# A linear-attention normaliser moved from TensorE products to VectorE block transposes

## The chip, the cores and the metric

The kernel runs on one core of one Trainium2 chip. The metric is the device time of the slowest core, here the only one, in microseconds (us). PE is TensorE, PEld its weight loads, DVE VectorE, ACT ScalarE, POOL GpSimd, SP SyncE.

## The reference, cut to what matters

```python
qkv = (x @ wqkv) ...                     # 32 heads of 16, S = 2048, D = 512
pq, pk = phi(q), phi(k)                  # phi(t) = where(t > 0, t + 1, exp(t)) + 1e-6
kv = einsum("bhsd,bhse->bhde", pk, v)
z = einsum("bhsd->bhd", pk)
num = einsum("bhqd,bhde->bhqe", pq, kv)
den = einsum("bhqd,bhd->bhq", pq, z)[..., None] + 1e-6
a = (num / den) ... @ wo
b = ...                                  # token-mixing MLP: layernorm, w1, gelu, w2
return g * a + (1 - g) * b               # g = sigmoid((x * gate_w).sum(-1))
```

The change touches `den`: one number per head and query. It is the sum of 16 products, the 16 features of that head times the head's column of sums `z`.

## The kernel before

All large products go through PE. Their names in the profile are `kacc` and `qacc` (k and q), `gacc` (phi(k)^T x), `uacc` (the first MLP product, 14 f-tiles of 16 matmuls), `aps` (attention output, 4 matmuls a tile of 128 queries) and `yps` (second MLP product, 14 a tile). Between two uacc f-tiles three short groups run: `kvps` (kv), `denps` (the normaliser) and `w2ps` (kv times Wo).

`pqT` holds phi(q) with features on the partitions, in four feature blocks j and four chunks c of 512 queries. The normaliser is a product with a masked column of sums, `Z32`. Its reciprocal then has to be spread from one row per head to 16 rows, and that was done by a round trip through DRAM:

```python
    def den_matmuls():
        denps = bank("denps")
        for j in range(ND):
            for c in range(NSC):
                mm(denps[32 * c : 32 * c + 32, :], Z32[:, 32 * j : 32 * j + 32],
                   pqT[:, j, c * SC : (c + 1) * SC],
                   j == 0, j == ND - 1, tile_position=(0, 32 * c))
        with nc.allow_low_precision(reason="the normalizer is used in bf16"):
            nc.vector.reciprocal(out=rden[:], in_=denps[:])
    ...
    def rden_chunk(c):
        if c == 0:
            nc.gpsimd.dma_start(out=rd_dram[:], in_=rden[:])
        for j in range(ND):
            rex = work.tile([P, SC], BF16, name="rex", tag="rex", bufs=4)
            src = rd_dram[32 * c + 8 * j : 32 * c + 8 * j + 8, :]
            nc.gpsimd.dma_start(out=rex[:], in_=src.unsqueeze(1).to_broadcast([8, HEAD, SC]))
            seg = pqT[:, j, c * SC : (c + 1) * SC]
            nc.vector.tensor_tensor(out=seg, in0=seg, in1=rex[:], op=ALU.mult)
    ...
    for j in range(NB0, NF):            # f-tiles 3 to 13
        ...                             # 16 uacc matmuls, then gelu on ACT
        if j == NB0 + 3:
            kv_matmuls(); den_matmuls(); w2_matmuls()
            gate_sums(); rden_chunk(0); rden_chunk(1)
        if NB0 + 3 <= j < NB0 + 3 + ND:
            w2_copies(j - NB0 - 3)
    ...
    for t in range(NT):                 # 16 tiles of 128 queries
        ...                             # aps, a_sc (ACT), yps, ot (DVE)
        (nc.scalar if t < 2 else nc.sync).dma_start(out=o_view[:, t, cs], in_=ot[:, :W])
        if 0 < t < NSC - 1:
            rden_chunk(t + 1)
```

`w2_matmuls` needs `kvT`, which DVE makes from `kvps` (a masked copy). PSUM has eight banks in this kernel's pool, two per tile in the last stage.

## Time and profile before

| | before |
|---|---|
| time, median of 3 runs | 164.11 us (164.09 to 164.12) |
| span of the profiled run | 162.3 us |
| PE / DVE / ACT busy | 97% / 55% / 39% |

The page of the kernel before: the line of busy times (engine, us, share of the span, instructions) and the shares by engine of the chain that ended last.

```profile
PE 157.7 (97%) x819; PEld 72.2 (45%) x833; DVE 90.0 (55%) x211; ACT 62.8 (39%) x96; POOL 17.5 (11%) x34
...
PE 94%; DMA 3%; issue 1%; ACTq 1%; DVE 0%
```

PE is busy nearly all the time (97%), and nearly the whole chain is PE (94%). A change elsewhere can be expected to gain nothing by itself.

The chain of waits of the kernel before, where the short groups run (start us, us, what):

```profile
66.26 4.91 PE uacc L113 x22
71.17 0.59 PE kvps L113 x64
71.76 0.88 PE denps L113 x16
72.65 0.36 PE w2ps L113 x16
73.01 0.32 PE uacc L113
```

PE leaves uacc at 71.17 and is back at 73.01. The 16 denps matmuls take 0.88 us of that. `kvT` is made meanwhile, so w2ps need not wait for it.

The groups of instructions of the kernel before on DVE that serve to cost the change (line, engine, operation, tile, shapes, count, busy us, mean ns, idle time before it):

```profile
L446 DVE TENSOR_TENSOR pqT<-pqT,rex 128x512 bf16<-128x512 bf16 x16 | 6.2, 421 | 3.9 <-DMA rex<-rd_dram 3.7
...
L404 DVE RECIPROCAL rden<-denps 128x512 bf16<-128x512 f32 x1 | 3.4, 3358 | 0.5 <-PE denps L113 0.5
...
L355 DVE STREAM_TRANSPOSE zT<-zacc 128x512 f32<-128x512 f32 x1 | 0.7, 711 | 0.0
L356 DVE TENSOR_REDUCE zpart<-zT 128x16 f32<-128x512 f32 x1 | 0.7, 686 | 0.0
```

A 128x512 fp32 block transpose and a sum over short runs are already in the kernel, once each. They give 711 and 686 ns for the new code, which does each 16 times. The reciprocal over 512 columns takes 3358 ns.

### The profile page before, as it was taken

How to read it: one execution, taken by the hardware profiler on the slowest of the kernel's cores; microseconds unless marked ns; L12 is line 12 of the kernel's file. 1: busy time of each engine (PE TensorE's matmuls, PEld its weight loads, DVE VectorE, ACT ScalarE, POOL GpSimd, SP SyncE). 2: the span in 40 equal slices, each digit the busy share in tenths (PEclk: the TensorE clock that was granted, in tenths of full speed). 3: DMA queues.
4: the chain of work that ended last, by engine and by line, in shares of the span. 5: the costliest groups of instructions: out<-in, count | busy, mean ns of one | idle time of the engine just before them, and what ended most of it. 6: DMA issues, size and time to landing. Idle time of an engine off the chain costs nothing.

```text
span 162.3 us, 2175 instructions
## 1 busy us (share of the span) xinstructions
PE 157.7 (97%) x819; PEld 72.2 (45%) x833; DVE 90.0 (55%) x211; ACT 62.8 (39%) x96; POOL 17.5 (11%) x34
## 2 busy tenths in 40 slices
PE   7999999999999999999999999999999999999993
PEld 3344444444444444444444444444444444444452
DVE  1799999957999999519995301256211111111112
ACT  3362486648676483112865113111222222111110
POOL 3000710200100000001505500050000000000000
DMA  5999999999900007500892599832000001110001
GB/s 149 203 249 259 288 295 352 377 387 387 345 18 0 0 0 247 205 4 0 290 316 86 203 299 324 298 129 72 32 32 32 32 32 43 48 42 33 32 32 32
DMA packets 30569, 25.18 MB, mean 155 GB/s; under 512 B 8480, under 2 KB 29984, under 8 KB 30560
## 3 DMA queue, kind: packets, MB, share of 16 engines
q1 hardware_dynamic: 28256, 21.89, 43.3%
q0 software_dynamic: 1440, 2.38, 5.5%
q10 hardware_dynamic: 864, 0.79, 1.5%
q8 instruction: 6, 0.10, 0.2%
q14 instruction: 3, 0.02, 0.0%
HBM read 21.11 MB, written 2.23 MB: 144 GB/s over the span
## 4 chain that ended last, share of the span: by engine, by line
PE 94%; DMA 3%; issue 1%; ACTq 1%; DVE 0%
PE uacc L113 30%; PE yps L113 30%; PE aps L113 8%; PE qacc L113 8%; PE gacc L113 8%; PE kacc L113 8%; DMA wk_sb<-in_A_wqkv_dram 3%; PE denps L113 1%; ACTq L129 1%; PE kvps L113 0%; PE w2ps L113 0%; DVE ot L505 0%; PE pt L335 0%
## 5 line engine op out<-in xcount | busy, mean ns | idle before, releaser
L113 PE MATMUL uacc<-hs,w1c 128*128 128x512 bf16 x220 | 51.1, 379 | 0.2
L113 PE MATMUL yps<-uT,w2c 128*128 128x512 bf16 (+2 forms) x234 | 50.6, 366 | 0.2
L505 DVE SCALAR_TENSOR_TENSOR ot<-yps,c,a_sc 128x512 bf16<-128x512 f32 (+2 forms) x17 | 12.2, 720 | 45.0 <-PE yps L113 41.8
L113 PEld LDWEIGHTS <-w2c 128*128 128x128 bf16 x238 | 22.8, 98 | 25.9
L113 PEld LDWEIGHTS <-w1c 128*128 128x128 bf16 x224 | 21.8, 98 | 26.3 <-issue 0.2
L492 ACT ACTIVATE a_sc<-aps,c,gg 128x512 f32<-128x512 f32 x16 | 12.4, 778 | 46.7 <-PE aps L113 39.9
L329 ACT ACTIVATE uT<-uacc,bcol 128x512 bf16<-128x512 f32 x14 | 9.3, 688 | 21.7 <-PE uacc L113 21.6
L113 PE MATMUL kacc<-wk_sb,xT 128*128 128x512 bf16 x63 | 16.1, 380 | 0.3
L113 PE MATMUL qacc<-xT,wq_sb 128*128 128x512 bf16 x61 | 16.1, 379 | 0.2
L113 PE MATMUL aps<-W2sb,pqT 128*128 128x512 bf16 x63 | 16.2, 379 | 0.1
L113 PE MATMUL gacc<-pk,xs 128*128 128x512 bf16 x63 | 15.6, 379 | 0.0
L256 ACT ACTIVATE hs<-xs,nmr,rstd 128x512 bf16<-128x512 bf16 x16 | 12.8, 805 | 1.8 <-DVE nmr L250 1.8
L216 ACT ACTIVATE e<-qacc 128x512 bf16<-128x512 f32 x16 | 9.6, 597 | 9.2 <-PE qacc L113 9.2
L216 ACT ACTIVATE e<-kacc 128x512 bf16<-128x512 f32 x16 | 9.3, 594 | 9.2 <-PE kacc L113 9.1
L444 POOL DMA_DIRECT2D rex<-rd_dram x16 | 9.5, 599 | 22.5 <-DVE pqT L446 19.4
L220 DVE SCALAR_TENSOR_TENSOR pk<-kacc,e 128x512 bf16<-128x512 f32 x16 | 11.1, 691 | 0.6
L220 DVE SCALAR_TENSOR_TENSOR pqT<-qacc,e 128x512 bf16<-128x512 f32 x16 | 11.1, 692 | 0.6
L113 PEld LDWEIGHTS <-xs 128*128 128x128 bf16 x76 | 7.2, 102 | 8.5 <-DMA xs<-in_A_x_dram 0.8
L240 DVE BATCH_NORM_STATS2 stats<-xs 128x6 f32<-128x512 bf16 x16 | 10.9, 682 | 0.0
L217 DVE TENSOR_SCALAR e<-e 128x512 bf16<-128x512 bf16 x32 | 9.0, 281 | 3.0 <-ACT e L216 3.0
L431 DVE CUSTOM_DVE_ANT_0 junk<-xs,gw_b 128x512 bf16<-128x512 bf16 x16 | 9.8, 681 | 0.0
L113 PEld LDWEIGHTS <-xT 128*128 128x128 bf16 x64 | 6.1, 97 | 8.2 <-DVE xT L212 0.6
(61 smaller groups left out, 73.0 us busy)
## 6 DMA issues: line engine op xcount, KB each, us to landing
w2c<-in_B_w_dram SPq DMA_DIRECT2D x8, 896.0 KB, 6.7
w1c<-in_B_w_dram SPq DMA_DIRECT2D x2, 2048.0 KB, 14.0
w1c<-in_B_w_dram SPq DMA_DIRECT2D x3, 1024.0 KB, 11.9
rex<-rd_dram POOLq DMA_DIRECT2D x16, 128.0 KB, 3.7
out_dram<-ot SPq DMA_DIRECT2D x13, 128.0 KB, 1.7
xs<-in_A_x_dram SPq DMA_DIRECT2D x3, 512.0 KB, 4.7
wq_sb<-in_A_wqkv_dram SPq DMA_DIRECT2D x1, 512.0 KB, 6.5
wv_sb<-in_A_wqkv_dram SPq DMA_DIRECT2D x1, 512.0 KB, 12.2
```

What stands on the lines that cost most here:

```text
L113: nc.tensor.matmul(o, lhsT=lhsT, rhs=rhs, start=start, stop=stop, **kw)
L129: q.dma_start(out=xs[:, t0 : t0 + n, :], in_=x_view[:, t0 : t0 + n, :])
L216: nc.scalar.activation(out=e[:], in_=acc[:], func=ACT.Exp)
L217: nc.vector.tensor_scalar(out=e[:], in0=e[:], scalar1=1.0, scalar2=PHI_EPS, op0=ALU.min, op1=ALU.add)
L220: nc.vector.scalar_tensor_tensor(out=dst, in0=acc[:], scalar=0.0, in1=e[:], op0=ALU.max, op1=ALU.add)
L240: nc.vector.bn_stats(out=stats[:], in_=xs[:, t, :])
L256: nc.scalar.activation(out=hs[:, t, :], in_=xs[:, t, :], func=ACT.Identity, scale=rstd[:, t : t + 1], bias=nmr[:, t : t + 1],)
L329: nc.scalar.activation(out=uT[:, j, :], in_=acc[:], func=ACT.Gelu_apprx_tanh, bias=bcol[:, j : j + 1])
L431: nc.vector.tensor_tensor_reduce(out=junk[:], in0=xs[:, t, :], in1=gw_b[:], scale=1.0, scalar=0.0, op0=ALU.mult, op1=ALU.add, accum_out=gp ...
L444: nc.gpsimd.dma_start(out=rex[:], in_=src.unsqueeze(1).to_broadcast([8, HEAD, SC]))
L492: nc.scalar.activation(out=a_sc[:], in_=aps[:], func=ACT.Identity, scale=gg[:, t : t + 1], bias=c2[:, t : t + 1],)
L505: nc.vector.scalar_tensor_tensor(out=ot[:, :W], in0=yps[:, :W], scalar=c1[:, t : t + 1], in1=a_sc[:, cs], op0=ALU.mult, op1=ALU.add,)
```

## The change

The intent is to take the normaliser off PE and off the DRAM round trip. ACT multiplies `pqT` by the column of sums, feature by feature. DVE transposes 32x32 blocks, so that the 16 features of a head lie side by side in one row; it sums runs of 16, takes the reciprocal of 32 columns, and transposes a broadcast view back, which spreads each reciprocal over 16 partitions. The work comes in 16 blocks (c, j): six during the uacc f-tiles and ten in the first ten query tiles. `kv_matmuls` moves one f-tile earlier, and `w2_matmuls` stays, now one f-tile behind it. The 16 gate sums on DVE, one block of work before, are spread over eight f-tiles, two in each.

```diff
-    def den_matmuls():
-        ...
+    def den_block(c, j):
+        seg = pqT[:, j, c * SC : (c + 1) * SC]
+        pz = work.tile([P, SC], FP32, name="pz", tag="pz", bufs=2)
+        nc.scalar.activation(out=pz[:], in_=seg, func=ACT.Copy, scale=zcol[:, j : j + 1])
+        nc.vector.transpose(out=zT[:], in_=pz[:])
+        den = work.tile([P, SC // HEAD], FP32, name="den", tag="den", bufs=1)
+        nc.vector.tensor_reduce(
+            out=den[:], in_=zT[:].rearrange("p (a d) -> p a d", d=HEAD), op=ALU.add, axis=AX.X
+        )
+        rd = work.tile([P, SC // HEAD], BF16, name="rd", tag="rd", bufs=1)
         with nc.allow_low_precision(reason="the normalizer is used in bf16"):
+            nc.vector.reciprocal(out=rd[:], in_=den[:])
+        rex = work.tile([P, SC], BF16, name="rex", tag="rex", bufs=1)
+        nc.vector.transpose(
+            out=rex[:].rearrange("p (a d) -> p a d", d=HEAD),
+            in_=rd[:].unsqueeze(2).to_broadcast([P, SC // HEAD, HEAD]),
+        )
+        nc.vector.tensor_tensor(out=seg, in0=seg, in1=rex[:], op=ALU.mult)
 ...
-        if j == NB0 + 3:
+        i = j - NB0
+        if i == 2:
             kv_matmuls()
-            den_matmuls()
+        elif i == 3:
             w2_matmuls()
-            gate_sums()
-            rden_chunk(0)
-            rden_chunk(1)
-        if NB0 + 3 <= j < NB0 + 3 + ND:
-            w2_copies(j - NB0 - 3)
+        if 3 <= i < 3 + ND:
+            w2_copies(i - 3)
+        if 2 <= i < 8:
+            den_block(*divmod(i - 2, ND))
+        if 2 <= i < 2 + NT // 2:
+            gate_sum(2 * i - 4)
+            gate_sum(2 * i - 3)
 ...
-        if 0 < t < NSC - 1:
-            rden_chunk(t + 1)
+        if t < NSC * ND - 6:
+            den_block(*divmod(t + 6, ND))
```

`Z32`, `rden`, the DRAM tile and its 17 transfers go.

More of the change, by code (lines that the diff above doesn't have):

```diff
@@ L63 @@
     opool = ctx.enter_context(tc.tile_pool(name="opool", bufs=4))
-    dpool = ctx.enter_context(tc.tile_pool(name="dpool", bufs=1, space=bass.MemoryType.DRAM))
     ps = ctx.enter_context(tc.tile_pool(name="ps", bufs=8, space=bass.MemoryType.PSUM))
@@ L84 @@
     W2sb = keep([P, ND, D], BF16, "W2sb")
-    Z32 = keep([P, ND * 40], BF16, "Z32")
     zacc = keep([P, D], FP32, "zacc")
@@ L91 @@
     zcol = keep([P, ND], FP32, "zcol")
-    rden = keep([P, SC], BF16, "rden")
     ident = keep([P, P], BF16, "ident")
@@ L146 @@
     nc.vector.memset(mhalf[:], -0.5)
-    nc.vector.memset(Z32[:], 0.0)
     nc.gpsimd.memset(ident[:], 0.0)
@@ L368, in z_column @@
             )
-        nc.vector.tensor_tensor(
-            out=Z32[:].rearrange("p (j m) -> p j m", m=40)[:, :, 0:8],
-            in0=zcol[:].unsqueeze(2).to_broadcast([P, ND, 8]),
-            in1=maskH[:].unsqueeze(1).to_broadcast([P, ND, 8]), op=ALU.mult,
-        )
     w2ps = []
@@ L393, in w2_copies @@
             )
-    def den_matmuls():
-        denps = bank("denps")
-        for j in range(ND):
-            for c in range(NSC):
-                mm(
-                    denps[32 * c : 32 * c + 32, :], Z32[:, 32 * j : 32 * j + 32], pqT[:, j, c * SC : (c + 1) * SC],
-                    j == 0, j == ND - 1, tile_position=(0, 32 * c),
-                )
-        with nc.allow_low_precision(reason="the normalizer is used in bf16"):
-            nc.vector.reciprocal(out=rden[:], in_=denps[:])
+    def den_block(c, j):
[8 more added lines that the diff above has]
+        rd = work.tile([P, SC // HEAD], BF16, name="rd", tag="rd", bufs=1)
+        with nc.allow_low_precision(reason="the normalizer is used in bf16"):
+            nc.vector.reciprocal(out=rd[:], in_=den[:])
[5 more added lines that the diff above has]
+        nc.vector.tensor_tensor(out=seg, in0=seg, in1=rex[:], op=ALU.mult)
     NB0 = 3
@@ L426, with gate_sum @@
     z_column()
-    def gate_sums():
-        for t in range(NT):
-            junk = work.tile([P, D], BF16, name="junk", tag="junk", bufs=2)
-            nc.vector.tensor_tensor_reduce(
-                out=junk[:], in0=xs[:, t, :], in1=gw_b[:], scale=1.0, scalar=0.0,
-                op0=ALU.mult, op1=ALU.add, accum_out=gpre[:, t : t + 1],
-            )
-    rd_dram = dpool.tile([P, SC], BF16, name="rd_dram", tag="rd_dram")
-    def rden_chunk(c):
-        if c == 0:
-            nc.gpsimd.dma_start(out=rd_dram[:], in_=rden[:])
-        for j in range(ND):
-            rex = work.tile([P, SC], BF16, name="rex", tag="rex", bufs=4)
-            src = rd_dram[32 * c + 8 * j : 32 * c + 8 * j + 8, :]
-            nc.gpsimd.dma_start(out=rex[:], in_=src.unsqueeze(1).to_broadcast([8, HEAD, SC]))
-            seg = pqT[:, j, c * SC : (c + 1) * SC]
-            nc.vector.tensor_tensor(out=seg, in0=seg, in1=rex[:], op=ALU.mult)
+    def gate_sum(t):
+        junk = work.tile([P, D], BF16, name="junk", tag="junk", bufs=2)
+        nc.vector.tensor_tensor_reduce(
+            out=junk[:], in0=xs[:, t, :], in1=gw_b[:], scale=1.0, scalar=0.0,
+            op0=ALU.mult, op1=ALU.add, accum_out=gpre[:, t : t + 1],
+        )
     w2c = []
```

## The prediction

> **What bounds the kernel.** TensorE. The page has PE busy 157.7 us of a 162.3 us span (97%), clock 1.00 in every window; the chain of waits is 94% PE, 3% the first weight DMA, 0-1% anything else. VectorE is 55% busy, ScalarE 39%, DMA light. So the change pays only where it shortens PE's instruction stream, and hurts only where a slower engine makes PE wait.
>
> **What PE gains.** In the chain of waits, PE leaves the uacc products at 71.17 us for kvps (64 matmuls, 0.59 us), denps (16, 0.88 us) and w2ps (16, 0.36 us), and is back at 73.01. The change deletes denps: -0.88 us. kv and w2 are now apart, with one 16-matmul uacc group between (about 3.45 us in the chain). That hides kvT (issued when kvps ends, 0.29 us on DVE), so w2ps should not wait. It costs one more switch between 128x128 products and narrow ones (four instead of three). The Trainium skill, "TensorEngine Tiling (Array Packing)", Key Properties, says that changing the tiling mode drains TensorE. A uacc matmul lasts 379 ns but follows the next at 0.86/4 = 0.215 us, so I estimate one more exposed drain at 0.15-0.3 us. Net: -0.6 us.
>
> **What moves, off PE.** Removed: a 3.36 us reciprocal, one store and 16 broadcast loads through DRAM on the POOL queue (2.1 MB, 3.7 us each to landing). No PE wait on them shows, so their removal is worth nothing directly. Added, 16 times: on ACT one fp32 product, estimated 0.7-0.8 us (hs, the like, takes 0.805); on DVE, estimated from the trace:
> - fp32 transpose 0.71 (zT 711 ns)
> - short sums 0.69 (zpart 686 ns; the skill's "VectorE: DVE Perf Modes", tier table, gives tensor_reduce one rate only)
> - reciprocal of 32 columns about 0.36 (rden: 3358 ns for 512)
> - bf16 transpose of the broadcast 0.71 (as the fp32 one)
> - multiply 0.42 (as now)
> Sum 2.9 us a block, 46 us in all; DVE busy about 90.0 - 3.5 + 16 x 2.47 = 126 us, near 77%. ACT about 75 us.
>
> **Does it reach the critical path?** I think not, narrowly.
> - Phase one (67.7 to 97 us): per uacc group DVE gets 2.9 + two gate sums (2 x 0.76) = 4.4 us against 3.45 us, so it falls behind for six groups, then has two groups of 1.5 us. Starting near 69 us it ends near 98.5-99. The gate tanh, 97.92 now, slips by about 1 us. The first ot needs yps only at about 100.6, and eight PSUM banks (two a tile) cover more.
> - Phase two: ot 0.75 + block 2.9 = 3.65 us per tile of 3.87-3.89 us, for tiles 0 to 9. It fits at about 94%. Chunk c is due at tile 4c; its last block is issued after tile 4c-3, so slack is about 4 us. PE would stall at blocks above about 3.5 us.
>
> **Prediction.** 163.5 us, range 162.9 to 164.3. Faster by over 2%: 1%; within 2%: 95%; slower by over 2%: 4%.
>
> **What would show it right.** denps gone from PE; PE busy down by about 1 us; kvps and w2ps 3.5-4 us apart; w2ps with no wait for kvT; no aps wait for pqT (chain of waits still PE at about 94%); DVE 75-80% with almost no idle from 69 to 98 us; phase two one aps+yps pair per 3.9 us, as before.
>
> **What would make it wrong.** The broadcast transpose or the short sums running well above 0.7 us: then phase two is paced by DVE and aps waits on pqT, costing up to several us, chiefly at tiles 8 and 12. A pz buffer (two) that stalls ACT, and so the gelu and a uacc bank. A drain as dear as denps: then the gain is nil.

## The result, and the profile after

The changed kernel takes 163.49 us (163.22 to 163.83, 4 runs). The kernel before took 164.10 us (164.01 to 164.12) in the same rounds. The ratio is 0.9965, with a 95% interval of 0.9945 to 0.9984. Ratios here are the mean time of one kernel's runs over that of the other's of the same rounds, so they are not quite the ratio of the medians. A repetition on another occasion gave 163.63 us and 0.9971 (0.9959 to 0.9983). The verdict is "same" at 2%, with a real gain of some 0.3 to 0.4%: both intervals lie below 1.

The page of the changed kernel, the same two lines:

```profile
PE 156.9 (97%) x802; PEld 72.1 (45%) x817; DVE 124.8 (77%) x272; ACT 72.8 (45%) x112; POOL 7.3 (4%) x17
...
PE 97%; DVE 1%; issue 1%
```

DVE went from 90 to 125 us busy. The 0.8 us between the two PE figures must not be read as the gain: some matmul records are missing from both traces (819 and 802 matmuls against 833 and 817 weight loads), and after_again, the same changed kernel with all 817 matmuls recorded, shows PE 158.1 us busy, more than the kernel before. The sure sign is the count of weight loads, which fell by the 16 of denps. The chain is still PE; how the remaining 3% at its start are attributed changes from run to run.

The chain of waits of the changed kernel, around the two short groups:

```profile
67.78 0.59 PE kvps L110 x64
68.37 0.32 PE uacc L110
...
68.74 3.19 PE uacc L110 x14
71.93 0.36 PE w2ps L110 x16
72.29 4.21 PE uacc L110 x19
```

The denps row is gone. kvps ends at 68.37, a whole uacc group runs, and w2ps follows it at 71.93 without any wait in the chain. Yet the timeline of the changed kernel has this line:

```profile
71.85 0.14 PEld L110 LDWEIGHTS <-kvT 32*32 32x32 bf16 x16 [0.42 <-DVE rex L399]
```

It seems to say that w2ps waited 0.42 us for DVE. That idle time belongs to the weight-load unit, which is busy for only 45% of the span, and its length is the same 0.42 us before the same loads in the kernel before. PE's own chain runs straight on from uacc to w2ps, so nothing was lost.

The groups of the new work in the changed kernel, in the columns of the groups of before:

```profile
L389 ACT ACTIVATE pz<-pqT,zcol 128x512 f32<-128x512 bf16 x16 | 11.4, 714 | 4.8 <-DVE ot L494 4.7
L399 DVE STREAM_TRANSPOSE rex<-rd 128x512 bf16<-128x512 bf16 x16 | 11.4, 711 | 0.6
L390 DVE STREAM_TRANSPOSE zT<-pz 128x512 f32<-128x512 f32 x16 | 11.3, 705 | 4.9 <-ACT pz L389 4.9
...
L392 DVE TENSOR_REDUCE den<-zT 128x32 f32<-128x512 f32 x16 | 11.0, 686 | 0.6
...
L403 DVE TENSOR_TENSOR pqT<-pqT,rex 128x512 bf16<-128x512 bf16 x16 | 6.8, 425 | 0.6
...
L397 DVE RECIPROCAL rd<-den 128x32 bf16<-128x32 f32 x16 | 5.6, 353 | 0.6
```

The estimates were right to a few ns: 0.71, 0.69, 0.36, 0.71 and 0.42 us were expected, and 705, 686, 353, 711 and 425 ns were found. The transpose of the broadcast operand took no longer than the fp32 transposes without one; a bf16 transpose without a broadcast was not run.

**Where the gain lies.** The start of this kernel scatters: in the kernel before, 4.20 us of the chain is the landing of the first weights, while in the changed kernel's trace the chain starts with PE's own first products. So I cut each trace at two points of the timeline view, the start of the first gacc product and the start of the first aps product. First the kernel before, then the changed kernel:

```profile
9.66 1.03 PE L113 MATMUL gacc<-pk,xs 128*128 128x512 bf16 x4
...
97.13 1.03 PE L113 MATMUL aps<-W2sb,pqT 128*128 128x512 bf16 x4
...
9.71 1.03 PE L110 MATMUL gacc<-pk,xs 128*128 128x512 bf16 x4
...
96.41 1.03 PE L110 MATMUL aps<-W2sb,pqT 128*128 128x512 bf16 x4
```

The middle stretch, from one trace of each kernel, is the same to 0.01 us in the eight traces whose kernels should not differ in it, and it tells kernels apart far more sharply than the times do. The views print the span to 0.1 us only; the last column takes the end of the last instruction from the packed trace.

| kernel | time, us (range) | ratio to before (95%) | first gacc to first aps, us | first aps to end, us |
|---|---|---|---|---|
| before | 164.11 (164.09 to 164.12) | 1 | 87.47 | 65.17 |
| changed | 163.49 (163.22 to 163.83) | 0.9965 (0.9945 to 0.9984) | 86.70 | 65.15 |
| after_again | 163.63 (163.46 to 163.71) | 0.9971 (0.9959 to 0.9983) | 86.70 | 65.16 |
| split_only | 164.31 (164.04 to 164.69) | 1.0015 (1.0002 to 1.0029) | 87.68 | 65.15 |
| den_back | 164.67 (164.33 to 165.10) | 1.0040 (1.0024 to 1.0055) | 87.67 | 65.15 |
| joined | 163.85 (163.78 to 164.11) | 0.9989 (0.9977 to 1.0001) | 87.10 | 65.14 |
| dma_back | 163.19 (163.10 to 163.62) | 0.9953 (0.9938 to 0.9968) | 86.69 | 65.16 |
| slow_half | 165.86 (165.80 to 166.55) | 1.0120 (1.0099 to 1.0141) | 86.69 | 67.44 |
| slow_half_sp | 163.82 (163.63 to 163.86) | 0.9983 (0.9964 to 1.0002) | 86.70 | 65.16 |
| slow_full | 169.62 (169.46 to 169.66) | 1.0338 (1.0321 to 1.0354) | 86.70 | 71.16 |
| slow_full_sp | 167.27 (167.10 to 167.53) | 1.0192 (1.0176 to 1.0209) | 86.69 | 68.60 |
| sp_stores | 163.35 (163.18 to 163.49) | 0.9952 (0.9940 to 0.9965) | 86.69 | 65.16 |

The change gains 0.77 us in the middle stretch and nothing after it (0.02 us). That is 0.47% of the time, a little more than the times of the changed kernel show; dma_back and sp_stores, with the same middle stretch, show 0.47 and 0.48%. In the traces of this table the first gacc starts between 9.59 and 9.96 us, so up to 0.4 us of the difference between two single runs is start-up. Only two traces have the old start (9.66 and 9.62 us), so whether the edit itself moves the start is not shown. The kernel before, run beside the experiments, ranged from 163.59 to 164.56 us.

### The profile page after: what moved, and what is told of

Its sections match the earlier page's. It is cut to its first block, busy times and chain, and to the rows that moved or that the text cites. A ratio compares the mean times of both kernels' runs of the same rounds, so it can differ in the third digit from the quotient of the medians.

```text
span 161.6 us, 2188 instructions
## 1 busy us (share of the span) xinstructions
PE 156.9 (97%) x802; PEld 72.1 (45%) x817; DVE 124.8 (77%) x272; ACT 72.8 (45%) x112; POOL 7.3 (4%) x17
## 4 chain that ended last, share of the span: by engine, by line
PE 97%; DVE 1%; issue 1%
PE uacc L110 30%; PE yps L110 30%; PE aps L110 9%; PE kacc L110 8%; PE qacc L110 8%; PE gacc L110 8%; PE wps L110 2%; PE pt L110 1%; DVE xT L208 0%; PE kvps L110 0%; PE w2ps L110 0%; DVE ot L494 0%; PE pt L331 0%
## 5 line engine op out<-in xcount | busy, mean ns | idle before, releaser
L390 DVE STREAM_TRANSPOSE zT<-pz 128x512 f32<-128x512 f32 x16 | 11.3, 705 | 4.9 <-ACT pz L389 4.9
L389 ACT ACTIVATE pz<-pqT,zcol 128x512 f32<-128x512 bf16 x16 | 11.4, 714 | 4.8 <-DVE ot L494 4.7
L399 DVE STREAM_TRANSPOSE rex<-rd 128x512 bf16<-128x512 bf16 x16 | 11.4, 711 | 0.6
L392 DVE TENSOR_REDUCE den<-zT 128x32 f32<-128x512 f32 x16 | 11.0, 686 | 0.6
```

The costliest lines, as they stand in the source:

```text
L389: nc.scalar.activation(out=pz[:], in_=seg, func=ACT.Copy, scale=zcol[:, j : j + 1])
L390: nc.vector.transpose(out=zT[:], in_=pz[:])
L392: nc.vector.tensor_reduce(out=den[:], in_=zT[:].rearrange("p (a d) -> p a d", d=HEAD), op=ALU.add, axis=AX.X)
L399: nc.vector.transpose(out=rex[:].rearrange("p (a d) -> p a d", d=HEAD), in_=rd[:].unsqueeze(2).to_broadcast([P, SC // HEAD, HEAD]),)
```

## The experiments

The theory is that PE's instruction stream alone decides. The 0.88 us of denps are gone, and one more switch between 128x128 products and narrow ones gives about 0.1 back. The rivals say that the gain comes from parting kv from w2, or from the vanished DRAM traffic, or is start-up scatter. A second set of runs tests how near DVE's new load is to stalling PE.

**after_again**: the changed kernel, unedited.

> The changed kernel again, to narrow its interval (first: ratio 0.9965, 0.9945 to 0.9984). Theory (the gain is denps leaving TensorE, less one dearer switch of array mode): 163.4 us, -0.7 us, ratio 0.9957. Rival (the gain is scatter of the kernel's start, as the runs of the changed kernel spread 163.22 to 163.83): ratio nearer to 1, 0.998 or more, with an interval that reaches 1.

Measured: 163.63 us, ratio 0.9971, interval 0.9959 to 0.9983. The interval does not reach 1, and the middle stretch is again 86.70 us. The gain is real, though a little smaller in time than expected (163.4). In the one run that was traced the first gacc came 0.2 us later than in the first trace; the other runs' starts are not on record.

**split_only**: the kernel before with kv one f-tile earlier, nothing else.

```diff
+        if j == NB0 + 2:
+            kv_matmuls()
         if j == NB0 + 3:
-            kv_matmuls()
             den_matmuls()
             w2_matmuls()
```

> The kernel before with its kv products moved one f-tile earlier and nothing else changed: den and w2 stay where they were. Theory: one more return to 128x128 products costs about 0.1 us, and the wait for kvT was hidden under the den products already, so +0.1 us (164.1 to 164.3). Rival (parting kv from w2 is the source of the gain, by hiding kvT): -0.4 to -0.6 us (163.5 to 163.7).

Measured: 164.31 us, at the upper edge of the expected range; middle stretch +0.21 us. The sign is the theory's and the rival is out, but the size is twice what I expected. The chain of waits of split_only shows why:

```profile
67.68 0.59 PE kvps L113 x64
68.28 3.56 PE uacc L113 x16
71.84 0.98 PE denps L113 x16
72.81 0.36 PE w2ps L113 x16
73.18 3.99 PE uacc L113 x18
```

The uacc group between takes 3.56 us and denps 0.98 us, where without a switch they take 16 x 0.2157 = 3.45 us (0.2157 us is the step from matmul to matmul: 14 yps take 3.02 us in the chain) and 0.88 us. Both have a switch of shape ahead of them. I had counted one additional switch where there are two: kvps and denps have the same 128x32 shape and followed each other without a switch before, and now there is one back to uacc and one to denps. Each costs about 0.10 us. Where the shape stays, nothing is added: the 4 aps and 14 yps of a query tile take 3.88 us, which is 18 x 0.2157.

**den_back**: the changed kernel with 16 products of the shape of denps put back, unused.

```diff
+    def den_products():
+        denps = bank("denps")
+        for j in range(ND):
+            for c in range(NSC):
+                mm(denps[32 * c : 32 * c + 32, :], ident[:, 0:32], xT[:, j, c * SC : (c + 1) * SC],
+                   j == 0, j == ND - 1, tile_position=(0, 32 * c))
 ...
+            den_products()
             w2_matmuls()
```

> The changed kernel, with 16 products of the same shapes as the removed den products (128x32 stationary, 512 columns) put back before w2; their sums are not used, so the result stays right. No DRAM round trip comes back. Theory: TensorE alone decides, so the 0.88 us return: +0.8 to +1.0 us against the changed kernel, 164.2 to 164.4, that is equal to or just above the kernel before. Rival (the gain is the DRAM round trip and the reciprocal gone): stays at 163.4 to 163.6.

Measured: 164.67 us, above the expected range, and 1.04 us above after_again in the same rounds. The middle stretch is +0.97 us against the changed kernel: 0.88 us of products and one more switch, as denps to w2ps is a change of shape too. In its chain of waits:

```profile
71.98 0.98 PE denps L110 x16
```

The whole gain is undone and slightly more, though the DRAM round trip and the long reciprocal are still gone. By this count the kernel equals split_only, which has both, and the two stretches agree (87.67 and 87.68). The median of den_back is 0.36 us above that of split_only all the same; as the two traces agree from the first gacc to the end, I put this down to the start, which one trace of each cannot show for the other runs.

**joined**: the changed kernel with w2 directly behind kv.

```diff
         if i == 2:
             kv_matmuls()
-        elif i == 3:
             w2_matmuls()
```

> The changed kernel with w2 directly behind kv, both two f-tiles behind the sums: no uacc group between. Theory: w2 now waits for kvT (its product ends, 0.29 us on DVE, and the way there and back: w2 starts about 0.5 us after kv ends), less one switch saved (0.1): +0.35 to +0.45 us against the changed kernel, 163.8 to 163.9. Rival (the distance between kv and w2 is worth nothing): 0 to -0.1 us, 163.3 to 163.5.

Measured: 163.85 us; middle stretch +0.40 us against the changed kernel, both as expected. The chain of waits of joined:

```profile
68.03 0.66 PE kvps L110 x64
...
68.71 0.30 DVE kvT L344
...
69.05 0.44 PE w2ps L110 x16
69.49 7.66 PE uacc L110 x35
```

Here, and only here, DVE's kvT stands in PE's chain, so the distance between kv and w2 does matter once denps no longer covers kvT. Moving kv forward was needed to keep the gain, not the source of it: without it 0.77 us would have been 0.37.

**dma_back**: the changed kernel with the removed traffic as a dead load.

```diff
+    def old_loads(c):
+        if c == 0:
+            nc.gpsimd.dma_start(out=rd_dram[:], in_=hs[:, 0, :])
+        for j in range(ND):
+            old = work.tile([P, SC], BF16, name="old", tag="old", bufs=1)
+            src = rd_dram[32 * c + 8 * j : 32 * c + 8 * j + 8, :]
+            nc.gpsimd.dma_start(out=old[:], in_=src.unsqueeze(1).to_broadcast([8, HEAD, SC]))
 ...
             w2_matmuls()
+            old_loads(0)
+            old_loads(1)
 ...
+        if 0 < t < NSC - 1:
+            old_loads(t + 1)
```

> The changed kernel, with the removed DRAM traffic put back as a dead load: one 128 KB store and 16 broadcast loads on the POOL queue into a tile that nobody reads (one buffer, as four no longer fit, so the loads follow one another). Theory: no wait of TensorE hangs on it, so 163.4 to 163.7, within 0.1 us of the changed kernel. Rival (the traffic or POOL's descriptor writing slowed something): 164.0 or more.

Measured: 163.19 us, and the middle stretch is 86.69 us, unchanged. The time is even below the changed kernel's, and below the expected range; as the traced run agrees with the changed kernel to 0.02 us from the first gacc on, its difference is in the start (first gacc at 9.59 us). Nothing here shows that the dead loads help. The rival is out as far as this test goes, but the test is not the old traffic in its old place: the dead loads wait for nothing that comes late, so POOL issues them one after another from 44.8 us to beyond 110 us, where before they went in bursts between 76 and 109 us. The stronger evidence is den_back against split_only: without and with the old traffic at its old density, the middle stretch is the same.

**slow_half** and **slow_full**: one needless transpose of 256, or of 512, columns in each block.

```diff
         nc.vector.transpose(out=zT[:], in_=pz[:])
+        nc.vector.transpose(out=zT[:, 0 : SC // 2], in_=pz[:, 0 : SC // 2])   # slow_half
+        nc.vector.transpose(out=zT[:], in_=pz[:])                             # slow_full
```

> The changed kernel with one needless fp32 transpose of 256 columns per block on DVE (about 0.44 us, 7 us in all; DVE would be about 81% busy). Theory (each chunk of pqT has a due time, and DVE with 0.66 + 2.93 us a tile has room for 0.29 us only): an addition by hand from the trace's durations, engine by engine in order, gives chunk 1's last block 1.9 us after TensorE wants it at tile 4, no wait later, so +1.9 us: 165.0 to 166.0. Rival (DVE at 77% has 37 us of idle time, so 7 us more are hidden): 163.4 to 163.7.

> As slow_half, with the full transpose repeated (about 0.74 us a block; DVE needs 4.33 us a tile against 3.88). The same addition by hand: waits for pqT at tiles 4, 8 and 12, in all +6 us: 168 to 171. Rival (hidden): 163.4 to 163.7. Rival (the added time shows in full): +12 us.

Measured: 165.86 us and 169.62 us; the last stretch is +2.29 and +6.01 us against the changed kernel. "DVE is only 77% busy, so more is hidden" is refuted. A share over the whole span says nothing of the stage in which DVE needs 3.59 us per tile against PE's 3.88. The weight loads that waited, in the timeline of slow_half:

```profile
113.32 0.10 PEld L110 LDWEIGHTS <-pqT 128*128 128x128 bf16 x1 [1.10 <-DVE pqT L404]
...
129.62 0.10 PEld L110 LDWEIGHTS <-pqT 128*128 128x128 bf16 x1 [1.07 <-DVE pqT L404]
...
145.91 0.10 PEld L110 LDWEIGHTS <-pqT 128*128 128x128 bf16 x1 [1.07 <-DVE pqT L404]
```

They are the last aps products of tiles 4, 8 and 12, one for each chunk of pqT. The bracket is the idle time of the weight-load unit; PE itself lost less. From the first aps of tiles 4, 8 and 12 to that of the next tile it takes 4.67, 4.64 and 4.64 us in place of 3.88, so the delays are 0.79, 0.76 and 0.76 us. My addition by hand gave about the right sum, +1.9 us, but put it all at tile 4, so that the sum came near was luck. I had made all four products of a tile wait for the chunk, while PE does the first three and waits only with the fourth. The delays at tiles 8 and 12 follow from the trace: DVE now needs 0.66 + 3.41 = 4.07 us a tile, PE 3.88, so over the four tiles between two chunks DVE loses 4 x 0.19 = 0.76 us, and once its room is spent PE loses it with DVE. The delay at tile 4 is nearly equal by chance, as something else comes in before it, which the chain of waits of slow_half shows:

```profile
108.61 0.35 ACTq L499
...
109.01 0.73 ACT pz L389
...
113.33 0.39 PE aps L110
```

Before tile 4 the chain runs through an output store on ACT's queue (L499) and the `pz` behind it; before tile 8 it stays on DVE, from `ot` at 125.41 to the transpose at 126.16. In slow_full the same three products wait longer:

```profile
114.90 0.10 PEld L110 LDWEIGHTS <-pqT 128*128 128x128 bf16 x1 [2.69 <-DVE pqT L404]
...
132.26 0.10 PEld L110 LDWEIGHTS <-pqT 128*128 128x128 bf16 x1 [2.13 <-DVE pqT L404]
...
149.62 0.10 PEld L110 LDWEIGHTS <-pqT 128*128 128x128 bf16 x1 [2.14 <-DVE pqT L404]
```

**slow_half_sp** and **slow_full_sp**: the same two, with all output stores issued by SP.

```diff
-            (nc.scalar if t < 2 else nc.sync).dma_start(out=o_view[:, t, cs], in_=ot[:, :W])
+            nc.sync.dma_start(out=o_view[:, t, cs], in_=ot[:, :W])
```

The reason for these runs is the ACT timeline of the changed kernel, around the first two output stores:

```profile
101.38 0.35 ACTq L498 DMA_DIRECT2D out_dram<-ot  x1
101.78 0.72 ACT L389 ACTIVATE pz<-pqT,zcol 128x512 f32<-128x512 bf16 x1 [1.22 <-DVE ot L494]
...
106.25 0.35 ACTq L498 DMA_DIRECT2D out_dram<-ot  x1
106.65 0.72 ACT L389 ACTIVATE pz<-pqT,zcol 128x512 f32<-128x512 bf16 x1 [3.48 <-DVE ot L494]
```

The kernel puts the store of tile 0 on ACT's queue ahead of `pz` of the next block. The store waits there for `ot`, and `pz`, which needs nothing of `ot`, starts only after it; the same happens with the store of tile 1. ACT is idle for 1.22 and 3.48 us. DVE then waits for `pz`, and chunk 1 comes closer to its due time. In the timeline of the changed kernel, the transpose of block 7 (the last of chunk 1), its multiply, and the first aps product of tile 4:

```profile
107.40 0.71 DVE L390 STREAM_TRANSPOSE zT<-pz 128x512 f32<-128x512 f32 x1 [1.18 <-ACT pz L389]
...
110.00 0.43 DVE L403 TENSOR_TENSOR pqT<-pqT,rex 128x512 bf16<-128x512 bf16 x1
...
111.95 1.03 PE L110 MATMUL aps<-W2sb,pqT 128*128 128x512 bf16 x4
```

The multiply ends at 110.43, 1.5 us before tile 4 starts (the fourth product, which needs this block, comes 0.65 us later). I had predicted about 4 us of room.

> As slow_half, but the first two output stores are issued by SP in place of ACT. In the changed kernel's trace the products pz of blocks 6 and 7 wait on ACT behind those stores, which wait for ot (1.2 and 3.5 us idle on ACT, 1.2 us each on DVE). Theory: that idle time returns, chunk 1 is in time, 163.4 to 163.8. Rival (only the sum of DVE's work counts, not the order on ACT's queue): as slow_half.

> slow_full with all output stores issued by SP. The addition by hand that gave +6.1 us for slow_full (measured 169.62, +6.1) gives +3.8 us here, as 2.4 us of DVE's idle time come back before tile 4: 167.0 to 167.8. Rival (the order on ACT's queue matters only near the edge): 169.6, as slow_full.

Measured: slow_half_sp takes 163.82 us with a last stretch of 65.16 us, so the whole stall of slow_half is gone with the same DVE work. (Its time is 0.02 us above the expected range; its traced run had the first gacc at 9.90 us.) slow_full_sp takes 167.27 us, as expected, +3.45 us in the last stretch where slow_full had +6.01. In the timeline of slow_full_sp the wait at tile 4 is gone and those at tiles 8 and 12 remain:

```profile
129.98 0.10 PEld L110 LDWEIGHTS <-pqT 128*128 128x128 bf16 x1 [1.95 <-DVE pqT L404]
...
147.34 0.10 PEld L110 LDWEIGHTS <-pqT 128*128 128x128 bf16 x1 [2.14 <-DVE pqT L404]
```

So the two idle times cost room that is spent at tile 4. Where DVE is slower than PE at each tile, better order on ACT's queue helped only once.

**sp_stores**: the changed kernel with all output stores on SP and nothing else.

> The changed kernel with all output stores issued by SP, none by ACT: nothing added. Theory: TensorE never waited, so the time stays (163.3 to 163.7), but DVE's idle time before blocks 6 and 7 (1.2 us each) goes, and chunk 1 is ready 2 us or more before its due time at tile 4 in place of 1.7 us after the trace of the changed kernel: about 3.5 to 4 us of room. Rival (ACT's stores were there for a reason: SP is busy with w2c loads and the first outputs come later, which holds up ot tiles): +0.3 us or more.

Measured: 163.35 us, both stretches as in the changed kernel (86.69 and 65.20). The last median is lower than the changed kernel's by 0.14 us, which is within the scatter of the start; I do not count it as faster. Its timeline, for the same multiply of block 7 and the same first product of tile 4:

```profile
107.61 0.42 DVE L403 TENSOR_TENSOR pqT<-pqT,rex 128x512 bf16<-128x512 bf16 x1
...
111.84 1.03 PE L110 MATMUL aps<-W2sb,pqT 128*128 128x512 bf16 x4
```

The multiply ends at 108.03, 3.8 us before tile 4. This is the version I would keep: the same time, with more than twice the room. Nothing in the runs points to a version that is clearly faster; of what PE does in the middle stretch beside its products, the four switches, of about 0.10 us where they could be measured, are the largest part that these runs made visible.

## Why the prediction was right

- **The size.** Predicted 163.5 us, range 162.9 to 164.3; measured 163.49 and 163.63. The mechanism was the predicted one: -0.88 us for denps plus one more switch. The net in the middle stretch was -0.77 us against a predicted -0.6, because the switch costs 0.10 us and not 0.15 to 0.3. split_only and den_back confirm the price from two sides. In the time, start-up scatter hid the difference; that the median fell within 0.01 us of the forecast is luck. The range also reached above the kernel before, so it would have held a kernel without any gain: the stretch and the experiments carry the mechanism, and the range does not.
- **The skill.** The Trainium skill, "TensorEngine Tiling (Array Packing)", Key Properties, says that a change of tiling mode drains TensorE. The traces agree that such a change costs time, about 0.10 us each; the drain itself they do not show. "VectorE: DVE Perf Modes", the perf-mode tier table, gives tensor_reduce one rate only, for bf16, fp32 and PSUM alike. Only fp32 in SBUF was run: 686 ns for sums over runs of 16 as over runs of 32. That fits one rate and does not test it across types.
- **DRAM traffic worth nothing.** Right: den_back against split_only, and dma_back.
- **w2ps without a wait.** Right, and by joined it is worth 0.40 us that kv was moved forward.
- **DVE's durations and its load.** 2.9 us a block was predicted. Measured from one block's first transpose to the next ot it is 2.93 us (111.01 to 113.94 in the timeline), and DVE's 77% was met.
- **Phase one.** The gate tanh was expected about 1 us later and came 1.06 us later (98.98 against 97.92). But DVE was not "almost without idle": the third block's transpose waited 1.74 us for its pz, which stood on ACT behind four W2sb copies (2.38 us). I had added up ACT's work and not followed its order.
- **The room.** This step of the prediction was wrong without consequence. "Slack is about 4 us" was 1.5 us, and "PE would stall at blocks above about 3.5 us" is too generous: slow_half's blocks of 2.93 + 0.48 = 3.41 us stalled PE by 2.29 us in all. The term I had left out is the two output stores on ACT's queue. With them on SP the room is 3.8 us, blocks of 3.41 us do not stall and the blocks of slow_full_sp, 3.68 us each (4.34 us a tile less 0.66 for `ot`), do, so the prediction's sum fits a kernel without that queue effect; the runs place its limit between the two and no closer.

## What to carry to other kernels

When one engine is saturated, the gain of a change is what leaves that engine's own stream, minus its added switches; here traffic of 2 MB and a 3.4 us reciprocal elsewhere counted for nothing, and 35 us more DVE work, in this order, cost nothing. Ask of the engine that takes over not how busy it is over the span, but when each result is due and what stands before it in every in-order queue on the way; a store that waits on a compute engine's queue can hold up what follows, here by 1.22 and 3.48 us. For differences below half a per cent, compare the stretch between two fixed points of the trace, which here repeated to 0.01 us where the start of the same work scattered by 0.4.

## What the Trainium skill lacked or had wrong

- "TensorEngine Tiling (Array Packing)", Key Properties: the drain at a change of tiling mode has no figure. Here a change from 128x32 or 32x32 products back to 128x128 cost 0.10 to 0.11 us, and one from 128x128 to 128x32 0.10 us (0.21 for two in split_only). The change into 32x32 could not be told from the products themselves.
- "VectorE: DVE Perf Modes", The three transpose paths: gives a time for one size only, 128x128 bf16. "Vector Engine (DVE) Microarchitecture Reference" has a rate for the transpose, but no time either. A 128x512 block transpose took 705 to 711 ns in fp32, one of 256 columns 446 ns (slow_half), so about 1.0 ns a column ((705 - 446) / 256); in bf16, with a source broadcast over 16 columns, 512 columns took 711 ns.
- "VectorE: DVE Perf Modes", the perf-mode tier table has no row for the reciprocal, and no page gives its time: 3358 ns for 512 columns out of PSUM and 353 ns for 32 out of SBUF, some 6.3 ns a column, if the fixed part is the same ((3358 - 353) / 480).
- "Trainium Kernel Development and Optimization", Key Constraints: it says that issuing DMAs from several engines only saves the sequencer's issue time. It lacks the price: two stores on ACT's queue held ACT's next product for 1.22 and 3.48 us and took 2.3 us of room from a chunk (3.8 against 1.5 us). "DMA: Bandwidth & Descriptors" has the wait on the issuing sequencer, but not what it holds up.
